# First batch prepared pair by pair with TensorE transposes inside its own attention block, later batches prepared ahead, written order, separate PSUM pools

## The chip, the cores and the metric

The kernel runs on one core of one Trainium2 chip. The metric is the device time of one execution in microseconds (us). Engines are named as the profile names them: PE (TensorE), PEld (its weight loads), DVE (VectorE), ACT (ScalarE), POOL (GpSimd) and SP (SyncE, which here issues DMAs). Sixteen DMA engines serve the core. "DMA share" is their mean busy share as the profile gives it; it reads a little over 1 at times.

## The reference, cut to what matters

Four batches, eight heads, 768 positions, head size 64. Each query and each key is assigned to the nearest of 16 centroids; attention is allowed only between positions of the same cluster. The result goes through a gated feed-forward layer.

```python
q_assign = argmax(q_n . c_n);  k_assign = argmax(k_n . c_n)      # per head, 16 clusters
scores = where(q_assign == k_assign, q @ k.T / 8, -1e9)
x = softmax(scores) @ v                                          # (4*768, 512)
out = (sigmoid(x @ w_gate) * (x @ w_val)) @ w_out                # d_ff = 1536
```

Inputs and outputs are float32; the kernel multiplies in float16.

## The kernel before

For every head q and k are turned so that the head dimension lies on the partitions ("T" below). Rows 0 to 63 hold the value, rows 64 to 127 first hold the rounding remainder (for exact cluster logits); then rows 64 to 79 are overwritten with a one-hot of the cluster times a large number, so that one matmul over 80 rows gives score and mask at once.

Preparing a batch means, for four pairs of heads and both sides: load, split into high and low half on DVE, transpose, cluster logits on PE, arg-max as a one-hot on DVE; then transpose and scatter the one-hots. All transposes are DMA transposes:

```python
def prep(b):                                   # cut
    for pr in range(NPR):                      # four pairs of heads
        for side in (1, 0):                    # k, then q
            ...                                # load q or k of the pair ("nat", 3 buffers)
            nc.vector.tensor_scalar(hl[:, :, 0, :], nat, SC, None, ALU.mult)
            nc.vector.scalar_tensor_tensor(hl[:, :, 1, :], nat, SC, hl[:, :, 0, :], ...)
            nc.sync.dma_start_transpose(out=T[b, side][...], in_=hl...)     # "hl": 3 buffers
            yield
            if side == 0:
                ...                            # 48 logit matmuls, max, one-hot; yields
    for side in (1, 0):
        nc.sync.dma_start_transpose(out=ohT, in_=ohf)
        for h in range(H):
            nc.sync.dma_start(out=T[b, side][D : D + NCL, h, :], in_=ohT[...])
```

Attention runs in eight blocks (four batches, two halves of the queries). A block has 24 steps (4 pairs x 6 key chunks). A step is two score matmuls, one exp of 128x768 on ACT, and six value matmuls. The feed-forward of the block before (132 matmuls) is mixed in, one generator step at a time. Scores, gate, value and output tiles share one ring of three two-bank PSUM buffers; the value accumulators have two banks.

```python
drain(prep(0))                                 # batch 0: everything before any attention
for i, (b, qb) in enumerate(blocks):
    if qb == 0 and b + 1 < B:
        prepg = prep(b + 1)
    for stepi, _ in enumerate(att(b, qb)):
        ...                                    # some of ffn(previous block)
        if prepg is not None and stepi % 2 == 0:
            next(prepg)                        # most of the next batch within block qb == 0
                                               # (stepi counts half steps here)
```

The softmax here doesn't subtract the row's maximum and nothing guards it: scores larger than these inputs give would overflow.

## Time and profile before

| | us |
|---|---|
| median of the runs before the prediction | 476.06 (471.02 to 478.19) |
| start to the first score matmul | 92 |
| eight blocks (between the transposes of the attention output) | 41, 41, 64, 42, 50, 40, 37.3, 37.3 |
| tail (last feed-forward and stores) | 32 |

The profiled execution took 477.74 us, about 1% above the fast runs (471 to 476 us).

The page's timeline of 40 slices of 11.9 us each gives the shape: digits are tenths of a slice in which the engine was busy.

```profile
...
PE   0000213178969991399999995999999999999996
...
PEclk9999999555559997599999997999999999999999
DMA  8999998479791079970051099002300300300301
...
```

For seven slices PE does almost nothing while the DMA engines are busy for eight tenths or more; the blocks follow. The next view gives busy microseconds of each engine by stretch, then the granted clock, the DMA share and the rate. The stretches shown are the start, the first block of batch 1 and the last block, which has no preparation in it.

```profile
...
core 0: us, PE busy (x) PEld busy (x) DVE busy (x) ACT busy (x) POOL busy (x), PEclk, DMA share, GB/s
0.00:92.00 92.00, 9.48 (x207) 7.68 (x208) 26.50 (x50) 1.49 (x2) 14.98 (x24) 0.96 1.04 179
...
174.30:238.00 63.70, 43.40 (x494) 26.86 (x491) 25.79 (x50) 26.77 (x38) 11.29 (x14) 0.84 0.67 130
...
406.80:444.10 37.30, 36.98 (x325) 21.77 (x324) 9.40 (x20) 27.55 (x39) 3.30 (x4) 1.00 0.12 33
...
```

The start is DMA-bound (share 1.04, PE busy 9.5 of 92 us). The second stretch is 63.7 us long with PE busy 43.4; the last is PE-bound (36.98 of 37.30). What the long second stretch waits for is in the chain of waits, in order of time (start, length, what):

```profile
...
176.96 20.03 DMA T_1517<-hl
...
```

That is one DMA transpose that lands 20 us after its issue, while loads of the next pairs and the 1.5 MB v load run.

### The profile page before, as it was taken

To read this page: it belongs to the slowest core of one execution; us is meant where nothing else is said; L and a number is where in the kernel's file an instruction comes from. 1 tells how busy PE (TensorE), PEld (TensorE's weight loads), DVE (VectorE), ACT (ScalarE), POOL (GpSimd) and SP (SyncE) were. 2 spreads that over 40 slices of the span, in tenths; PEclk is the share of its full clock that TensorE was granted. 3 is DMA by queue.
4 is the path that set the end of the run, shared out by engine and by line. 5 is a ranking of instruction groups with operands and counts; after the bars stand their busy time and mean duration, and the time that the engine had idled before them with its cause. 6 is when DMAs were issued, how large, how long until landed. Compare 5 with 4: busy or idle time off the path is not lost.

```text
span 476.0 us, 8217 instructions
## 1 busy us (share of the span) xinstructions
PE 348.2 (73%) x3410; PEld 209.5 (44%) x3410; DVE 154.5 (32%) x310; ACT 227.8 (48%) x315; POOL 64.5 (14%) x83
## 2 busy tenths in 40 slices
PE   0000213178969991399999995999999999999996
PEld 0000112044546650256566643665665565565562
DVE  4001522535533361263313253433223123032140
ACT  1000000066547760156658752665686787687331
POOL 2300020314220150030101040100000000010000
PEclk9999999555559997599999997999999999999999
DMA  8999998479791079970051099002300300300301
GB/s 259 148 110 178 235 219 161 114 132 246 214 170 39 3 156 211 155 222 23 3 124 43 1 168 264 2 2 36 103 30 1 101 2 1 99 1 2 101 0 66
DMA packets 83749, 49.32 MB, mean 104 GB/s; under 512 B 71296, under 2 KB 76352, under 8 KB 83712
## 3 DMA queue, kind: packets, MB, share of 16 engines
q1 hardware_dynamic: 76800, 28.32, 33.3%
q0 software_dynamic: 6768, 20.45, 18.0%
q8 instruction: 26, 0.43, 0.4%
q14 instruction: 11, 0.09, 0.1%
q10 hardware_dynamic: 144, 0.03, 0.0%
HBM read 28.34 MB, written 6.29 MB: 73 GB/s over the span
## 4 chain that ended last, share of the span: by engine, by line
PE 52%; DMA 26%; ACT 9%; DVE 5%; issue 4%; SPq 4%; POOL 0%; ACTq 0%; DVEq 0%; POOLq 0%
PE ring L311 19%; PE ring L277 13%; PE ring L328 10%; ACT es L285 8%; DMA nat<-in_q_dram 5%; PE av L240 5%; DMA T_1517<-hl 4%; DMA T_144<-hl 4%; PE ring L161 3%; DMA T_464<-hl 2%; SPq L146 2%; DMA T_462<-hl 2%; DMA T_142<-hl 2%; DVE hl L142 2%; PE ring L212 2%
## 5 line engine op out<-in xcount | busy, mean ns | idle before, releaser
L285 ACT ACTIVATE es<-ring,nbias 128x768 f16<-128x768 f32 x192 | 172.3, 900 | 99.4 <-PE ring L277 93.8
L311 PE MATMUL ring<-xT,wg 128*128 128x384 f16 x384 | 97.0, 331 | 6.0 <-DMA xT<-x 3.5
L311 PE MATMUL ring<-xT,wv 128*128 128x384 f16 x384 | 92.9, 329 | 0.0
L321 DVE SCALAR_TENSOR_TENSOR hT<-g,ring 128x384 f16<-128x384 f32 x96 | 53.2, 554 | 108.9 <-ACT g L320 107.8
L240 PEld LDWEIGHTS <-es 128*128 128x128 f16 x1152 | 62.5, 103 | 34.0 <-ACT es L285 9.7
L328 PE MATMUL ring<-wo,hT 128*128 128x512 f16 x288 | 76.6, 382 | 0.0
L240 PE MATMUL av<-va,es 128*128 128x65 f16 x1152 | 72.8, 202 | 2.0 <-ACT es L285 1.6
L262 POOL TENSOR_TENSOR x<-avs,ri 128x384 f16<-128x384 f32 x32 | 27.8, 867 | 243.3 <-DVE ri L261 193.3
L320 ACT ACTIVATE g<-ring 128x384 f32<-128x384 f32 x96 | 46.5, 484 | 10.9 <-PE ring L311 10.5
L311 PEld LDWEIGHTS <-wg 128*128 128x128 f16 x384 | 34.9, 98 | 24.9 <-issue 7.8
L285 ACT ACT_TABLE_LOAD x1 | 1.3, 1283 | 89.8 <-PE ring L277 89.8
L311 PEld LDWEIGHTS <-wv 128*128 128x128 f16 x384 | 34.6, 98 | 17.5 <-issue 1.0
L277 PE MATMUL ring<-T_142,T_144 80*128 80x384 f16 x96 | 33.0, 445 | 11.3 <-DMA T_142<-ohT_431 11.0
L142 DVE TENSOR_SCALAR hl<-nat 128x768 f16<-128x768 f32 x32 | 18.6, 585 | 55.7 <-DMA nat<-in_q_dram 27.8
L143 DVE SCALAR_TENSOR_TENSOR hl<-nat,hl 128x768 f16<-128x768 f32 x32 | 36.3, 1136 | 0.6
L250 DVE TENSOR_TENSOR avs<-av,sv 128x390 f32<-128x390 f32 x32 | 18.0, 564 | 56.0 <-PE av L240 56.0
L328 PEld LDWEIGHTS <-hT 128*128 128x128 f16 x288 | 25.6, 98 | 20.2
L337 ACT ACTIVATE osb<-ring 128x512 f32<-128x512 f32 x24 | 14.3, 595 | 41.6 <-PE ring L328 41.2
L161 PE MATMUL ring<-cT,T_144 128*128 128x16 f16 x96 | 3.2, 175 | 38.9 <-DMA T_144<-hl 38.9
L173 DVE TENSOR_REDUCE mx<-ring 128x12 f32<-128x192 f32 x32 | 11.3, 353 | 61.5 <-PE ring L161 61.5
L277 PE MATMUL ring<-T_462,T_464 80*128 80x384 f16 x96 | 24.1, 333 | 0.9 <-ACT es L285 0.3
L277 PE MATMUL ring<-T_1517,T_1519 80*128 80x384 f16 x96 | 24.1, 332 | 0.6
(68 smaller groups left out, 192.9 us busy)
## 6 DMA issues: line engine op xcount, KB each, us to landing
vn<-in_v_dram POOLq DMA_DIRECT2D x4, 1536.0 KB, 13.4
out_dram<-osb SPq DMA_DIRECT2D x24, 256.0 KB, 2.4
nat<-in_k_dram POOLq DMA_DIRECT2D x12, 384.0 KB, 5.2
nat<-in_q_dram POOLq DMA_DIRECT2D x12, 384.0 KB, 5.8
nat<-in_k_dram SPq DMA_DIRECT2D x4, 384.0 KB, 5.5
nat<-in_q_dram SPq DMA_DIRECT2D x4, 384.0 KB, 4.3
wg<-in_moe_w_gate_dram POOLq DMA_DIRECT2D x1, 1536.0 KB, 18.4
wv<-in_moe_w_val_dram POOLq DMA_DIRECT2D x1, 1536.0 KB, 26.3
```

Source lines behind the costliest of these rows:

```text
L142: nc.vector.tensor_scalar(hl[:, :, 0, :], nat, SC, None, ALU.mult)
L143: nc.vector.scalar_tensor_tensor(hl[:, :, 1, :], nat, SC, hl[:, :, 0, :], ALU.mult, ALU.subtract)
L161: nc.tensor.matmul(out=cl[:, sd, o : o + NCL], lhsT=T[b, sd][:, h, bass.ts(c, 128)], rhs=cT[:, r, bass.ts(h, NCL)], start=(r == 0), stop=( ...
L240: nc.tensor.matmul(out=av[:, o : o + D + 1], lhsT=es[:, hh, bass.ts(t, 128)], rhs=VA[b][:, 2 * pr + hh, j, :], start=(j == 0 and hh == 0 a ...
L250: nc.vector.tensor_tensor(s, av[:, 0 : 2 * QCH * (D + 1)].rearrange("p (h t d) -> p h t d", h=2, t=QCH), SV[b][:, 2 * pr : 2 * pr + 2, :] ...
L262: nc.gpsimd.tensor_tensor(x[:, :, 2 * pr * D : 2 * (pr + 1) * D].rearrange("p t (h d) -> p h t d", h=2), s[:, :, :, 0:D], ri.unsqueeze(3). ...
L277: nc.tensor.matmul(out=sc[:, hh, 0:QB], lhsT=T[b, 1][0 : D + NCL, h, bass.ts(j, 128)], rhs=T[b, 0][0 : D + NCL, h, bass.ts(qb, QB)], start ...
L285: nc.scalar.activation(es, sc[:, :, 0:QB], AF.Exp, bias=nbias, scale=es_scale)
L311: nc.tensor.matmul(out=gv[:, i, 0:QB], lhsT=w[:, dc, bass.ts(fc, 128)], rhs=xT[:, :, dc, :], start=(dc == 0), stop=(dc == NDC - 1),)
L320: nc.scalar.activation(g, gv[:, 0, 0:QB], AF.Tanh, scale=0.5)
L321: nc.vector.scalar_tensor_tensor(hT[:, fc, :], g, 1.0, gv[:, 1, 0:QB], ALU.add, ALU.mult)
L328: nc.tensor.matmul(out=o[:, 0, :], lhsT=hT[:, fc, bass.ts(t, 128)], rhs=wo[:, fc, :], start=(fc == 0), stop=(fc == NFC - 1),)
```

## The change

The intent, as the diff shows it: let attention start as soon as one pair of heads is ready. Batch 0 is turned by PE transposes, pair by pair, the later three pairs inside block 0. Batches 1 to 3 keep DMA transposes, but spread over both blocks of the batch before, with eight steps between a transpose and the logits that read it. All engines take instructions in written order (no reordering by the scheduler). PSUM is divided: two two-bank score buffers, three one-bank buffers, one value bank. Smaller edits go with it: three SBUF pools ("oh", "sm", "g") lose one buffer each, and the last feed-forward may use the score buffers too.

```diff
+    ctx.enter_context(tc.manual_schedule())
-    natp = ... bufs=3        +    natp = ... bufs=4
-    ring = PSUM bufs=3 (two banks each); avp = PSUM bufs=2
+    scp = PSUM "sc" bufs=2 (two banks each); fp_ = PSUM "f" bufs=3 (one bank); avp = PSUM bufs=1
...                                            (loads of q, k, v now all from SyncE)
+    def prep_pe(pr):                          # batch 0, one pair; a generator
+        for side in (1, 0):
+            hl = split(b, side, pr)
+            pt = scp.tile([128, 2, 1024], HP, name="sc")
+            for hh in range(2):
+                for c in range(NCH):
+                    nc.tensor.transpose(pt[:, hh, bass.ts(c, 128)], hl[...], ident)
+                yield
+            # evict: k on DVE, q on ACT
+            ...
+        for side in (1, 0):
+            logits(b, side, pr); onehot(...); scale
+            yield
+        for side in (1, 0):
+            po = scp.tile([128, 2, 1024], HP, name="sc")
+            ...                                # transpose the one-hots too, evict 16 rows
...
+    def plan(b):
+        for pr in range(NPR):
+            a = 6 + 8 * pr                     # steps 0 to 47 of the batch before
+            at(max(a - 9, 0), load_pair, b, pr)
+            at(a, prep_a, b, pr)               # splits and DMA transposes
+            at(a + 8, prep_b, b, 1, pr)        # logits and one-hot
+            at(a + 9, prep_b, b, 0, pr)
+        at(16, load_v, b); at(25, prep_v, b); at(34, prep_sv, b)
+        at(40, prep_oh, b, 1); at(41, prep_oh, b, 0)
...
-    drain(prep(0))
+    for _ in prep_pe(0):
+        pass
+    load_v(0); prep_v(0); load_weights()
```

## The prediction

> **What bounds the kernel now.** I cut the span at the eight attention-output transposes (timeline: issued at 133, 174, 238, 280, 330, 369, 407 and 444 us). Before the first score matmul at 92 us the tensor engine is busy 9.5 us of 92 and the DMA share is 1.04 (stage windows): the prologue is DMA-bound. The float32 loads, the weights, eight DMA transposes of q and k (landing in 10 to 16 us median, one 35 us) and the one-hot scatter (16 issues of 0.6 us) all stand before any attention. Then blocks take 41, 41, 64, 42, 50, 40, 37.3 and 37.3 us, and the tail 32 us. The last two blocks have no preparation and are TensorE-bound (busy 0.99). The 64 and 50 us blocks are those into which the whole preparation of the next batch is packed: 178 to 216 us has DMA share 1.01, TensorE busy 18.6 of 38, one transpose landing after 20 us.
>
> **What the change does.**
> - Prologue: only pair 0 is prepared. Chain by durations in the trace: load lands 4.8; centroids to about 7; splits 0.56+0.96 each side; transposes about 1.5 a side; evictions about 1 us on VectorE, 1.6 on ScalarE (estimates from the 256-column copy, 0.29, and the 768-column exp, 0.90); logits 0.8; one-hot about 1.1; second transposes and evictions 3. Attention starts at about 20 us, not 92: -72 us. Eight pair transposes and two one-hot transposes (with xT and the other batches about 158 us of all 16 engines for 44 equivalents, so 3.6 us each: 32 us) leave the busiest DMA stretch.
> - Block 0 becomes heavier. It carries three pair preparations (144 transposes, 6 evictions on ScalarE), all in written order with two score buffers, and half of batch 1. The granted clock was 0.5 in block 0 before; there a score pair cost 0.64 us, the six value matmuls 0.51. The Trainium skill ("TensorE: Matmul & The Clock Gate", Part 4) says that transposes do not count as busy for the clock; no trace here shows it yet. At half clock: attention 27.7 + transposes about 17 + logits and sums about 11 = 56 us. The weights (issued only after the v casts, about 31 us) and batch 1's transposes contend, and TensorE waits in order. I expect block 0 to take about 57 us (40 to 70), ending at about 77: +16.
> - Later batches: spread over 48 steps, transposes 8 steps ahead. The 64 and 50 us blocks become about 42: -30. Other prepared blocks stay at 41 to 44; one-channel waits (3 us VectorE splits ahead of the gate product, one value buffer, one-hot scatter close to the batch boundary) cost a few us each.
> - Last two blocks and tail: unchanged, 75 + 32, perhaps 1 us less.
>
> **Sum.** 77 + 44 + 4 x 42.5 + 75 + 32 = 398 us. Nearly all the gain is on the critical path, since nothing ran beside the prologue.
>
> Predicted 397 us, 80% range 372 to 425. Faster by over 2%: 0.96; within 2%: 0.03; slower: 0.01.
>
> **What would show each step.** First exp at 18 to 24 us; clock 0.5 through block 0 with TensorE busy most of it; weights landing before the first gate matmul (about 84 us); batch-1 logits in block 0 waiting for transposes by 0 to 10 us; no block of batches 1 and 2 over 45 us; DMA share under 0.7 after 120 us; last blocks 37 to 38 us; tail 32 us.
>
> **What would make it wrong.** Block 0 warm (then about 375); or batch-1 transposes and pair-3 loads starved behind the weights (SyncE issues in order), or written order stalling TensorE on VectorE bursts by several us per pair in every batch (then 420 and more).

## The result, and the profile after

The changed kernel takes 412.94 us (median of 4 runs, 411.72 to 414.36) against 474.06 us before (median of 4, 471.02 to 478.19; the ratio below leaves out the 478.19, which is over 1.5% above the fastest). Ratios here and below are the mean time of one kernel's fast runs over that of the other's fast runs of the same rounds, so they are not quite the ratio of the medians: 0.873, 95% interval 0.866 to 0.880. Of the changed kernel the profiled one spans 411.4 us.

The same rows of the page, now with slices of 10.3 us:

```profile
...
PE   1675956888899989989998989988999999999996
...
PEclk9968586569999999999999999989999999999999
DMA  5589998433116936740129476330230003000301
...
```

The same view of the changed kernel, with the start, block 0, the second block of batch 2, and the last block.

```profile
...
0.00:19.10 19.10, 7.47 (x98) 6.69 (x99) 9.74 (x23) 4.72 (x5) 2.77 (x10) 1.00 0.60 208
19.10:82.60 63.50, 45.51 (x604) 34.34 (x604) 34.20 (x64) 32.45 (x33) 8.90 (x11) 0.67 0.87 197
...
257.10:303.50 46.40, 42.47 (x433) 25.78 (x431) 16.32 (x36) 27.56 (x40) 6.20 (x7) 0.96 0.23 60
...
341.20:379.70 38.50, 36.82 (x326) 21.77 (x324) 9.41 (x20) 27.35 (x39) 3.29 (x4) 1.00 0.11 33
...
```

The account of the two profiled runs, with the first exp as the end of the start (95.7 us before, 21.0 us after), in us:

| | before | after | difference |
|---|---|---|---|
| to the first exp | 95.7 | 21.0 | -74.7 |
| block 0 | 37.5 | 61.5 | +24.0 |
| block 1 | 41.0 | 43.9 | +2.9 |
| batch 1 | 63.7 + 42.1 | 42.2 + 45.6 | -18.0 |
| batch 2 | 49.5 + 39.8 | 42.8 + 46.4 | -0.1 |
| batch 3 | 37.3 + 37.3 | 37.7 + 38.5 | +1.6 |
| tail | 31.9 | 31.7 | -0.2 |

The start gives 75 us and block 0 takes back a third of it. The 64 us block is gone, but batch 2 gains nothing: what its first block wins, its second loses. The last blocks, which the change was not about, are a little longer (1.6 us over both, and the profile before was itself a slow one).

Three kinds of lines tell about the losses. First the chain of waits through block 0:

```profile
...
37.28 0.51 PE sc L194 x6
...
41.17 0.37 SPq L76
...
41.59 14.72 DMA T_295<-hl
...
56.41 0.57 DVE hl L150
...
58.02 0.60 PE sc L194 x6
...
```

A DMA transpose of batch 1, issued in the middle of block 0, lands after 14.7 us; DVE's next split waits for its buffer; PE's next transposes wait for that split. But a long piece on the chain is not its cost. The list of waits shows how long DVE was really idle for this buffer (total us, times, longest):

```profile
...
DVE hl L150 <- DMA T_295<-hl: 1.2, 1, 1.2
...
```

It was only 1.2 us, because DVE had other work of the block until just before: a second path, nearly as long, ran beside the transpose. Second, who PE waited for in block 0 (total us, times, longest), and third, in the last block:

```profile
...
PE sc L194 <- DVE hl L151: 8.5, 4, 3.5
PE sc L336 <- ACT T_153 L227: 4.3, 4, 1.6
PE f L165 <- DVE ohw L177: 3.0, 3, 1.8
...
```

```profile
...
PE av L299 <- DVE avs L309: 1.6, 3, 0.6
```

In block 0 PE waits for a split, an eviction or a one-hot in turn. In the last block it waits for DVE to empty the single value bank before the next pair may start.

### The profile page after: what moved, and what is told of

It is laid out like the page before. It is cut to its first block, busy times and chain, and to the rows that moved or that the text cites. A ratio compares the mean times of both kernels' runs of the same rounds, so it can differ in the third digit from the quotient of the medians.

```text
span 411.4 us, 8513 instructions
## 1 busy us (share of the span) xinstructions
PE 355.7 (86%) x3602; PEld 222.2 (54%) x3602; DVE 159.3 (39%) x327; ACT 237.3 (58%) x324; POOL 43.5 (11%) x56
## 3 DMA queue, kind: packets, MB, share of 16 engines
q1 hardware_dynamic: 72832, 40.12, 35.7%
## 4 chain that ended last, share of the span: by engine, by line
PE 57%; DVE 13%; ACT 11%; DMA 10%; issue 6%; SPq 0%; POOL 0%; ACTq 0%; DVEq 0%
PE f L376 18%; PE f L393 13%; PE sc L336 10%; ACT es L344 7%; PE av L299 6%; DMA T_295<-hl 4%; DVE avs L309 3%; PE f L165 3%; DVE hl L150 3%; ACT g L385 3%; DVE hl L151 3%; DMA out_dram<-osb 2%; PE sc L376 2%; PE f L273 2%; PE sc L194 1%
## 5 line engine op out<-in xcount | busy, mean ns | idle before, releaser
L344 ACT ACTIVATE es<-sc,nbias 128x768 f16<-128x768 f32 x192 | 172.3, 900 | 122.1 <-PE sc L336 117.5
L386 DVE SCALAR_TENSOR_TENSOR hT<-g,f 128x384 f16<-128x384 f32 x90 | 49.8, 554 | 135.5 <-ACT g L385 107.8
L376 PE MATMUL f<-xT,wg 128*128 128x384 f16 x360 | 92.7, 329 | 5.2 <-ACT g L385 3.6
L376 PE MATMUL f<-xT,wv 128*128 128x384 f16 x360 | 87.5, 327 | 3.2 <-ACT g L385 2.0
L393 PE MATMUL f<-wo,hT 128*128 128x512 f16 x288 | 75.7, 379 | 0.0
L385 ACT ACTIVATE g<-f 128x384 f32<-128x384 f32 x90 | 43.5, 483 | 3.6 <-PE f L376 3.6
L336 PE MATMUL sc<-T_153,T_154 80*128 80x384 f16 x96 | 30.4, 410 | 5.4 <-ACT T_153 L227 4.3
L176 DVE TENSOR_REDUCE mx<-f 128x12 f32<-128x192 f32 x32 | 11.3, 352 | 48.9 <-PE f L165 48.9
L336 PE MATMUL sc<-T_1737,T_1739 80*128 80x384 f16 x96 | 24.0, 330 | 0.2 <-DMA T_1737<-ohT_2879 0.2
L336 PE MATMUL sc<-T_3046,T_3048 80*128 80x384 f16 x96 | 23.5, 325 | 0.2 <-DMA T_3046<-ohT_4188 0.2
L336 PE MATMUL sc<-T_293,T_295 80*128 80x384 f16 x96 | 23.6, 325 | 0.0
L402 ACT ACTIVATE osb<-f 128x512 f32<-128x512 f32 x24 | 14.2, 593 | 14.3 <-PE f L393 12.0
L194 PE MATMUL sc<-ident,hl 128*128 128x128 f16 x96 | 10.5, 273 | 12.7 <-DVE hl L151 12.2
## 6 DMA issues: line engine op xcount, KB each, us to landing
wv<-in_moe_w_val_dram POOLq DMA_DIRECT2D x1, 1536.0 KB, 20.2
wo<-in_moe_w_out_dram POOLq DMA_DIRECT2D x1, 1536.0 KB, 31.7
```

The lines of the kernel that those rows point to most:

```text
L194: nc.tensor.transpose(pt[:, hh, bass.ts(c, 128)], hl[:, hh * NCH + c, :, :].rearrange("p a d -> p (a d)"), ident,)
L336: nc.tensor.matmul(out=sc[:, hh, 0:QB], lhsT=T[b, 1][0 : D + NCL, h, bass.ts(j, 128)], rhs=T[b, 0][0 : D + NCL, h, bass.ts(qb, QB)], start ...
L344: nc.scalar.activation(es, sc[:, :, 0:QB], AF.Exp, bias=nbias, scale=es_scale)
L376: nc.tensor.matmul(out=gv[i][:, 0:QB], lhsT=w[:, dc, bass.ts(fc, 128)], rhs=xT[:, :, dc, :], start=(dc == 0), stop=(dc == NDC - 1),)
L385: nc.scalar.activation(g, gv[0][:, 0:QB], AF.Tanh, scale=0.5)
L386: nc.vector.scalar_tensor_tensor(hT[:, fc, :], g, 1.0, gv[1][:, 0:QB], ALU.add, ALU.mult)
```

## The experiments

All kernels gave the right result except the one marked. The "kernel before" ran on the same chip: 469 to 486 us, slow runs included. The changed kernel itself was not run again, so a run is compared with its 412.94 us; differences of about 1% (4 us) in the total are near the noise of that comparison. My theory was first that the gain is the start, less what block 0 pays back, plus the unpacking of batch 1. Rivals: the written order or the pools make the gain; and for block 0: half clock, DMA contention, or handovers between engines.

### 1. Batch 0 by DMA transposes, up front

```diff
-    for _ in prep_pe(0): pass
-    load_v(0); prep_v(0); load_weights()
+    load_v(0); prep_v(0); load_weights()
+    for pr in range(NPR):
+        prep_a(0, pr); ...                     # load pair pr + 2, logits of pair pr - 1
+    ...; prep_oh(0, 1); prep_oh(0, 0); prep_sv(0)
     # and no prep_pe inside block 0
```

> The changed kernel with one part undone: batch 0 is prepared before attention by DMA transposes again, all four pairs; written order, pools and the spread of later batches stay. My theory (the gain is the prologue, 92 to 19 us, less 22 us that block 0 pays back): first exp at 80 to 95 us, block 0 at 38 to 46 us, total 450 to 470 us. Rival (written order and the separate PSUM pools make the gain): total below 425 us.

Measured: 436.85 us (one of the four runs, 445.27, was slow), ratio 0.927 (0.921 to 0.932). The first exp came at 72.1 us, block 0 took 33.7 us. Both fell outside what I had written, and the total lies between the two theories.

So pair-by-pair preparation on PE is worth 24 us (437 to 413), not the whole gain: attention starts 51 us earlier, block 0 is 28 us longer. The other 24 us of the earlier start come from the rest of the change, since the same DMA transposes now end at 72 us instead of 96. The chain of this start still consists of DMA:

```profile
...
15.11 8.10 DMA T<-hl
...
28.57 22.15 DMA T<-hl
...
```

Which difference (written order, loads from SyncE with four buffers, weights issued after v instead of at 2.6 us) makes those 24 us was not separated.

This run also shows a trap. Its granted-clock row is nines throughout, yet its score pairs in block 0 take as long as at half clock:

```profile
...
PEclk9999999999999999999999999999999999999999
...
```

```profile
...
97.87 0.83 PE L336 MATMUL sc<-T,T 80*128 80x384 f16 x2
...
```

The trace holds the changes of the clock, and the first record of this run comes only after block 0. Before the first record the row reads as full and means nothing; a duration tells (a score pair takes 0.83 us at half clock, 0.49 at full).

### 2. Without the written order

```diff
-    ctx.enter_context(tc.manual_schedule())
```

> The changed kernel without the written order (the scheduler may reorder again), nothing else. My theory: the written order is not where the gain comes from, total 400 to 425 us. Rival: written order is needed for it, total 435 us or more.

Measured: 408.39 us, ratio 0.867. The written order is not needed for the gain. The kernel seems even about 1% faster without it (405.7 to 409.9 against 411.7 to 414.4 us), but the intervals of the two ratios overlap. Its first exp is later (29.3 us) but its last two blocks take 35.6 us, and PE has no recorded wait in them:

```profile
...
338.70:374.30 35.60, 35.60 (x326) 21.74 (x324) 9.42 (x20) 27.36 (x39) 3.29 (x4) 1.00 0.12 35
...
```

That is less than the 37.3 us of the kernel before as well. So something else in the change shortens these blocks, most likely the separate pools (argued, not tested alone), and the written order takes it back.

### 3. The kernel before with its preparation spread out

```diff
-            if prepg is not None and stepi % 2 == 0:
+            if prepg is not None and (stepi + 49 * qb) % 3 == 0:
```

> The kernel before, where the next batch's preparation advances at every third half step through both blocks instead of every second half step of the first. My theory (batch 1's 64 us block was DMA-bound packing): the 64 us and 49 us blocks fall to 42 to 48, the second blocks rise by 2 to 4, total 448 to 462 us. Rival (the gain in batch 1 came from the written order, or from the start of the kernel): total 468 us or more.

Measured: 467.40 us as the median of the three fast runs (464.69 to 468.36), ratio 0.992 (0.985 to 0.999). I had expected at most 462; this is a miss, and the total is close to what the rival said. The profiled execution fell into a slow state (525 us, clock 0.81), so its block lengths can't be compared with the others. Its order of work can: about three fifths of the next batch's logit matmuls lie in the first block of batch 1 instead of nine tenths, so the edit did spread the preparation. Spreading alone, without the lead of eight steps between transpose and logits, is worth about 1% in the old kernel.

### 4. Both splits of a pair first

```diff
         for side in (1, 0):
-            hl = split(b, side, pr)
+        hls = {side: split(b, side, pr) for side in (1, 0)}    # ahead of the loop
```

> The changed kernel with both splits of a pair written ahead of the first transposes in the pair preparation. If block 0 is long because TensorE waits in order for VectorE's split (8.5 us of such waits in block 0, four times): these waits fall below 3 us, block 0 from 63 to 55 to 60 us, total 404 to 410 us. Rival (half clock, or DMA contention, bounds block 0): 411 to 414 us.

Measured: 411.96 us, ratio 0.875; block 0 63.1 us. No gain, as the rival said. The split waits fell from 8.5 to 2.3 us, but the time came back elsewhere:

```profile
...
PE av L300 <- DVE avs L310: 8.1, 4, 5.0
...
PE sc L195 <- DVE hl L151: 2.3, 1, 2.3
...
```

DVE now stood earlier behind the same late DMA transpose (16.3 us on this run's chain) and the value evictions stood behind DVE. That made me suspect the contention with the weights.

### 5. No weight loads (wrong result)

```diff
-        nc.gpsimd.dma_start(out=wg, in_=moe_w_gate...)      # the same for wv and wo
+        nc.gpsimd.memset(wg, 0.03)
```

> The changed kernel with the three weight loads replaced by memsets (wrong result on purpose). New theory after the first four runs: block 0 is held up by batch 1's first DMA transpose, which lands after 14.7 us because the weights share the DMA engines, and keeps its split buffer, so VectorE waits in written order. Then block 0 falls from 61 to 46 to 54 us and the total to 396 to 406. Rival (half clock and TensorE-VectorE handover alone bound block 0): block 0 stays above 58 us, total above 408.

Measured: 426.92 us, ratio 0.903; block 0 took 74.2 us, longer than with the weights. The experiment brought in a cost of its own. In the order of time on DVE and on POOL:

```profile
...
16.86 0.56 DVE L150 TENSOR_SCALAR hl<-nat 128x768 f16<-128x768 f32 x1
...
21.68 15.35 DVE L150 TENSOR_SCALAR hl<-nat 128x768 f16<-128x768 f32 x1
...
```

```profile
...
21.09 5.21 POOL L130 MEMSET wg<- 128x6144 f16 x1
26.24 5.21 POOL L131 MEMSET wv<- 128x6144 f16 x1
31.41 5.21 POOL L132 MEMSET wo<- 128x6144 f16 x1
...
```

A split that takes 0.56 us took 15.35, just as long as the three memsets ran. The Trainium skill, page "SBUF — State Buffer", section "Who interferes with whom", says that tensor_scalar on DVE can use a mode that needs the port pair which DVE shares with GpSimd, and that whoever comes first blocks the other. This trace agrees: the first memset began at 21.09 us, the split at 21.68. Less the 14.8 us of that split, block 0 would be about 59 us (an estimate), hardly shorter than 61.5. What the run does show is what makes the transpose late: without the weights no DMA transpose of q or k took more than 4.9 us to land, against 14.7. So the late transpose is on the chain, but removing the load that delays it does not seem to shorten the block; because of the side effect I count this as a hint, not as a proof.

### 6. Six split buffers

```diff
-    hlp = ... bufs=3
+    hlp = ... bufs=6
```

> The changed kernel with six split buffers instead of three; nothing else. Buffer theory: the split for pair 3 no longer waits for the transpose of batch 1 to let go of its buffer: block 0 falls by 4 to 10 us, total 402 to 409. Rival (contention itself: the logits of batch 1 then wait for the same late transpose in TensorE's written order): less than 2 us, total 411 to 414.

Measured: 413.51 us, ratio 0.874; block 0 61.2 us. No gain. The DMA transpose left block 0's chain altogether, but the length stayed, as the wait of only 1.2 us would lead one to expect: a chain of handovers took its place.

```profile
...
46.92 0.79 PE f L165 x24
...
48.36 1.28 PE sc L218 x12
...
49.97 1.30 PE sc L218 x12
51.35 1.43 ACT T L227
52.80 0.91 ACT es L344
...
53.76 0.80 PE sc L194 x6
...
```

Here logits, transposes of the one-hots, the eviction, an exp, and only then the next pair's transposes follow one another: transposes and scores take turns on the same two buffers.

### 7. Batches 2 and 3 packed again

```diff
-            a = 6 + 8 * pr                    # logits at a + 8, a + 9
+            a, d = (6 + 8 * pr, 8) if b == 1 else (4 * pr, 4)   # logits at a + d, a + d + 1
```

> The changed kernel with the preparation of batches 2 and 3 packed into four steps per pair in the first block of the batch before (transposes four steps ahead of their logits), as dense as in the kernel before; batch 1 stays as it is. If the spread is what removed the 64 and 50 us blocks: the blocks 42.2 and 42.8 rise by 5 to 20 us each while the blocks after them fall by 3 to 5, total 418 to 440. Rival (those blocks were long for another reason): total 408 to 416.

Measured: 433.24 us, ratio 0.919, as expected. Both first blocks became long again while the blocks after them lost 3 to 4 us:

```profile
...
126.50:182.40 55.90, 44.23 (x511) 27.12 (x507) 26.30 (x52) 26.87 (x39) 3.35 (x6) 0.91 0.62 164
182.40:225.00 42.60, 39.68 (x346) 23.42 (x345) 10.80 (x24) 28.62 (x41) 6.18 (x7) 1.00 0.22 47
225.00:280.80 55.80, 44.37 (x512) 27.30 (x510) 26.30 (x52) 26.88 (x39) 3.29 (x5) 0.91 0.65 164
...
```

So spread with lead is worth 20 us (433 to 413) within the changed kernel. Spread and lead were changed together here; run 3 suggests that spread alone is the smaller part, but it ran in another kernel.

### 8. Written order for the start and block 0 only

```diff
-    ctx.enter_context(tc.manual_schedule())
+    written = ExitStack(); written.enter_context(tc.manual_schedule())
...
             prev = (b, qb)
+            if b == 0 and qb == 0:
+                written.close()
```

> Written order for the start and block 0 only; from block 1 on the scheduler may reorder. In the run without written order the last two blocks took 35.6 us with TensorE busy all the time, against 37.7 and 38.5 in written order, but its first exp came at 29 us against 21. If both read right: block 0 ends near 82.5 us as in the changed kernel, later blocks are 1 to 7 us shorter each, total 394 to 402. Rival (the shorter blocks came from the different state after its start): 407 to 414.

Measured: 400.65 us (400.24 to 400.88), ratio 0.847: faster than both kernels. The last two blocks took 35.7 and 35.6 us and the second block of batch 2 39.6 instead of 46.4. Written order costs the changed kernel 12 us in blocks 1 to 7.

### 9. Batch 1's work moved out of block 0

```diff
-            a = 6 + 8 * pr
+            a, d = (6 + 8 * pr, 8) if b > 1 else (24 + 4 * pr, 4)
...
-        at(40, prep_oh, b, 1); at(41, prep_oh, b, 0)
+        at(41, prep_oh, b, 1); at(42, prep_oh, b, 0)
```

> The changed kernel with batch 1's splits, transposes and logits moved out of block 0 into block 1 (four steps a pair there). If batch 1's share of the work is what makes block 0 long: block 0 falls from 61 to below 50 us; block 1 rises by about 13 us, as the packed blocks did. If it is the handover between engines inside each pair's preparation: block 0 stays at 54 to 60 us. Total 412 to 424.

Measured: 424.71 us, ratio 0.898. The total is 0.7 us above the range. Block 0 took 55.3 us, within the range for handovers, and block 1 53.2. Batch 1's share of block 0 is worth 6 us, not more. The edit had a side effect: the one-hot scatter starts one step later in all batches, and the second blocks of batches 1 and 2 rose from 45.6 and 46.4 to 50.1 and 49.4 us; at the end of one of them PE waited 2.7 us for the last scatter. SyncE needs about 16 us for the two one-hot transposes and 16 scatters, and in the changed kernel they end just in time.

### 10. Own banks for the transposes

```diff
-            pt = scp.tile([128, 2, 1024], HP, name="sc")     # both heads, then evict
-            for hh in range(2):
+            for hh in range(2):
+                pt = fp_.tile([128, 1024], HP, name="f")      # one head, evict at once
...                                            (the same for the one-hot transposes)
```

> The changed kernel with the pair preparation's transposes going to the three single-bank buffers, which stand idle in block 0, head by head, instead of taking the two score buffers. If block 0 is long because transposes and scores take turns on two buffers: block 0 falls from 61 to 48 to 56 us, total 398 to 408. Rival (the half clock, or VectorE alone): block 0 stays above 58 us, total 409 to 414.

Measured: 411.52 us, ratio 0.873; block 0 60.7 us. No gain either, and the other chain is back:

```profile
...
40.58 14.54 DMA T<-hl
...
55.21 0.57 DVE hl L150
...
```

### 11. Keeping the clock up

```diff
+                if b == 0 and qb == 0:
+                    wm = fp_.tile([128, 512], FP, name="f")
+                    for _ in range(2):
+                        nc.tensor.matmul(out=wm, lhsT=ident, rhs=zz, start=True, stop=True)
```

> The changed kernel with two spare matmuls of 512 columns at each of the 48 half steps of block 0, into a bank nobody reads, to keep the granted clock up; they add about 20 us of TensorE work at full clock and 41 at half. If the half clock is what makes block 0 long: the clock is 1.0 through it and block 0 falls by 5 us or more. Rival (handovers): block 0 within 3 us of 61 or longer although the clock is up.

Measured: 415.53 us, ratio 0.881; block 0 62.0 us. The same stretch, first of the changed kernel, then of this one:

```profile
...
20.00:82.50 62.50, 44.54 (x595) 33.50 (x592) 34.20 (x64) 32.15 (x33) 8.04 (x10) 0.67 0.88 199
...
```

```profile
...
20.00:82.50 62.50, 52.70 (x693) 34.10 (x692) 33.91 (x64) 31.83 (x33) 7.11 (x10) 0.97 0.89 198
...
```

The clock rose from 0.67 to 0.97 and the block did not become shorter. The spare matmuls themselves fill PE (52.7 us busy instead of 44.5), so a benefit of several us could hide behind them; the run alone does not exclude that. The profile of the changed kernel sets a limit: of the chain through the 61.5 us of block 0, pieces on PE make up only 16.3 us in sum (those on DVE 23.0, the DMA piece 14.7), so full clock could save at most half of that, about 8 us (an estimate). The half clock is a part of block 0's length at most, not the main part.

### 12. Both limits lifted at once

Run 6 took away the late transpose and found a chain of handovers of the same length; run 10 moved the transposes off the shared score buffers and found the late transpose again. The last version lifts both, and takes what runs 4 and 8 offered: own banks for the transposes, six split and six load buffers, both splits first, batch 1's first split at step 9 instead of 6 (its logits three steps later too), and the scheduler from block 1 on.

```diff
   (the edits of 4, 6, 8 and 10)
-    natp = ... bufs=4
+    natp = ... bufs=6
-            at(a, prep_a, b, pr)
+            at(9 if (b, pr) == (1, 0) else a, prep_a, b, pr)
```

> A version meant to beat both kernels. Six split buffers alone gained nothing and own banks for the transposes gained nothing, each leaving the other limit on block 0's chain; here both are lifted at once, with both splits first, six load buffers and batch 1's first split moved three steps later, and the scheduler allowed to reorder from block 1 on (400.65 us by itself). If the two limits are parallel chains of about equal length: block 0 falls from 63 to 48 to 57 us and the total to 386 to 397 us. Rival (block 0 is bounded by work and handovers that none of these touch): block 0 stays above 59 us, total 398 to 403.

Measured: 381.40 us (6 runs, 380.67 to 383.20), ratio 0.811 (0.806 to 0.815). The total is below the range I gave.

```profile
...
16.00:74.80 58.80, 45.27 (x653) 34.10 (x654) 44.58 (x81) 38.26 (x46) 12.29 (x11) 0.76 1.04 236
...
201.30:236.20 34.90, 34.66 (x392) 22.14 (x391) 14.09 (x31) 24.92 (x37) 3.30 (x4) 1.00 0.50 102
...
311.40:347.10 35.70, 35.70 (x326) 21.80 (x324) 9.41 (x20) 27.40 (x39) 3.32 (x5) 1.00 0.12 35
...
```

The first exp comes at 17.2 us and block 0 ends at 74.8 us instead of 83.6 in run 8, 8.9 us of the 20.2 us between the two profiles. Block 0 itself takes 57.6 us, between the two theories and only 4 us less than in the changed kernel, so lifting the two limits did not free it. Its chain now holds a later DMA transpose and a load:

```profile
...
33.90 18.34 DMA T<-hl
...
56.80 7.75 DMA nat<-in_k_dram
...
```

The DMA engines are full over this stretch (share 1.04), and the transpose lands at 52.2 us, when the last weight load does (about 52). Yet PE waited only 0.3 us for it, and DVE 2.1 us for the load, so here too other work ran beside them nearly as long. What bounds block 0 at 57.6 us is open; the weights' traffic with both other limits lifted was not tested. The rest of the gain comes later, most of it in the first block of batch 2, which takes 34.9 us instead of 44.2; whether load buffers or split buffers do that was not tested. A version with two value banks and two instead of three one-bank buffers was not run, because it deadlocks when it is built and simulated, so what the single value bank costs by itself is open.

## Why the prediction was right or wrong

The predicted 397 us (372 to 425) stands against 412.94 measured: the direction, the size and the range hold, and the point was 16 us too low. That the number for block 0 came out near is partly luck, as its reason was not the right one.

- **Start.** "Attention starts at about 20 us, not 92: -72 us." The first score matmul came at 19.1 us and the first exp at 21.0. The chain of durations read from the trace was right. The attribution was not tested by the prediction, and run 1 shows that only 51 of the 75 us are owed to the PE transposes.
- **Block 0.** "I expect block 0 to take about 57 us (40 to 70), ending at about 77: +16." It took 63.5 us from the first score matmul and ended at 82.5. The size was near, the reason wrong: I costed it as PE work at half clock. PE was busy 45.5 of 63.5 us, the clock changed back and forth with a mean of 0.67 instead of staying at 0.5, and run 11 raised it without gain. Two paths of about equal length run through it: handovers PE to DVE or ACT and back over shared score buffers (run 6), and splits that wait for buffers held by DMA transposes that the weights delay (run 10). The prediction had named transposes starved behind the weights as a risk, but for PE's logits, which have no recorded wait for them in block 0; it was a split buffer that was held. Lifting one path alone gave nothing. Run 12 lifted both among other things and took only 4 us off block 0's 61.5, so the two paths are not the whole account; what the rest is stays open.
- **Clock and transposes.** The cited sentence that transposes do not count as busy is not borne out by this trace: the clock rose after a run that was mostly transposes, and transposes then ran at full clock (below).
- **Packed blocks.** "The 64 and 50 us blocks become about 42: -30." They became 42.2 and 42.8, and run 7 brought them back to 55.9 and 55.8.
- **Other prepared blocks.** The step that failed most: "Sum. 77 + 44 + 4 x 42.5" and "no block of batches 1 and 2 over 45 us". The second blocks took 45.6 and 46.4 us, so the four took 177 us instead of 170. Together with 5.5 us at the end of block 0 and 1.2 us in the last two blocks this makes 13.7 of the 16 us between prediction and measurement; the measured time is also 1.5 us above the profiled span, and the sum of 398 was stated as 397. The written order was named as a risk and it was one, at 12 us (run 8); I had counted "a few us each" only for some blocks.
- **Weights.** "Weights landing before the first gate matmul" was right: the last one was issued at 23.7 us and landed 31.7 us later, at about 55.
- **DMA.** "DMA share under 0.7 after 120 us" was slightly off: 0.73 and 0.71 in the first blocks of batches 1 and 2.
- **Last blocks and tail.** "75 + 32" against 76.2 and 31.7. I did not expect that they could be shorter: with separate pools and no written order they take 35.6.

## What to carry to other kernels

When work is moved from a serial start into a busy block, cost the block by its chain of handovers and its buffers, not only by the busiest engine. A long piece on the chain can cost far less than its length (14.7 us on the chain, 1.2 us of idle time behind it): where paths of about equal length run side by side, lifting one alone shows no gain, and lifting two need not free the block. Written order is useful where the scheduler picks badly (the start), and costs time where it could fill small waits; it can be limited to the part that needs it. Transfers that must land in time seem to need a lead as well as an even spread (runs 3 and 7; no run changed the lead alone), and a part of a change that looks like its heart can turn out to be two fifths of its gain (24 of 61 us).

## What the Trainium skill lacked or had wrong

- Page "TensorE: Matmul & The Clock Gate", Part 4, says that the full clock does not engage for transposes because they don't count as busy in the same way. In the changed kernel 24 logit matmuls and 24 transposes ran back to back for 3.3 us (2.69 us of it transposes), and after that twelve transposes took 0.83 us instead of 1.46. The run was not of transposes alone, but about four fifths of it were; so transposes do run at full clock here, while whether they alone raise it is not shown. On PE, in order of time:

```profile
...
7.23 1.46 PE L194 MATMUL sc<-ident,hl 128*128 128x128 f16 x12 [1.18 <-DVE hl L151]
...
14.21 0.80 PE L165 MATMUL f<-cT,T_153 128*128 128x16 f16 x24 [0.92 <-DVE ohw L177]
...
14.86 2.69 PE L218 MATMUL sc<-ident,ohw 128*80 128x128 f16 x24
...
19.45 0.83 PE L194 MATMUL sc<-ident,hl 128*128 128x128 f16 x12
...
```

- Page "SBUF — State Buffer", "Who interferes with whom": the shared port pair is said to be held for a whole instruction. In run 5 one 0.56 us split waited for three memsets in a row, 15.35 us; the page does not say that back-to-back instructions keep the lock.
- No page says how the time before a trace's first clock record is to be read. The profile used here shows it as full clock: in run 1 score pairs took 0.83 us under a row of nines.
- Page "DMA: Bandwidth & Descriptors", section "Latency and other measured facts", gives a rate for DMA transposes but not what happens beside other traffic: in the changed kernel the transposes of 128x1536 float16 landed after 3.5 us at the median, and at the longest after 14.7 us, beside the weights; without the weights (run 5) the longest took 4.9 us. In run 1 one piece of the chain was 22.15 us.
